# Masking of a key-value product: which side of the instruction has the stride

## The chip, the cores and the metric

The kernel runs on one core of one Trainium2 chip. The metric is the device time of one execution in microseconds; the time before is the median of three runs.

## What is computed

Two linear-attention blocks, A and B, read the same x (2048 rows of 640), and a gate mixes their outputs. There are 32 heads of width 20. Cut to what matters:

```
qkv = x @ wqkv                                     # per block, q, k, v of 32 heads
phi = lambda t: where(t > 0, t + 1, exp(t)) + 1e-6
pq, pk = phi(q), phi(k)
kv  = einsum("bhsd,bhse->bhde", pk, v)             # per head, 20 x 20
z   = einsum("bhsd->bhd", pk)
o   = einsum("bhqd,bhde->bhqe", pq, kv) / (pq . z + 1e-6)
out = g * (o_A @ wo_A) + (1 - g) * (o_B @ wo_B)    # g = sigmoid(sum(x * gate_w))
```

## The kernel before

All the work is listed as operations, each with an engine, a cost, its buffers and a priority, and a planner (`Sched`, from L105 on) lays them out by these costs; each engine then executes its list in that order, with semaphore waits between engines. The order of the PE products is written out by hand (`MAIN`), and the planner lets the query products fill in.

The kernel never forms v. It multiplies the key features with x itself (a matrix G of 640 x 640 for each block), and G with the value weights. The products of G and later those of the output use a scheme with seven half-size products for eight (steps numbered 1 to 7 in `MAIN`), so that the halves are combined by additions.

- **Keys** (L622, L623 on PE): projections of x, then exp and relu on ACT and the sum on DVE. L693 is one form of that sum: it reads PSUM as `p (m g) -> p g m` and writes runs of 128.
- **G** (`prod`, L889 on PE): five units G0 to G4. Each step is eight matmuls. ACT copies some results out (L918), DVE combines PSUM with a copy (`comb`, L923) into a tile, and writes the column for the denominator (`zsum`, L937, into `DEN`); its input is one float read 32 times, and it has a second scalar from PSUM. Step 4 of a unit writes into the bank that step 7's combine (called c22) and its z column have read, so it waits for both. A finished tile is transposed by a DMA of SP's queue into `GSA` or `GSB`.
- **Key-value product** (`kv_unit`, from L1003 on): for each block, matmuls (L1031) multiply the transposed G with the value weights. One result of a group of six heads has their value columns on its partitions and their 120 key columns along the row (24 values of m times 5 of g, key column 5m + g); of it only the blocks of a head with itself are wanted, so the mask depends on the partition and on m (the last group has two heads, 40 columns). DVE multiplies the PSUM result with a mask of zeros and ones (L1011) and writes the tile `KVL` in bf16. That is three instructions for each block: 480 elements a partition (four groups), 120 (one group) and 40 on 40 partitions.
- **Combined weights** (`wp_burst`, L1064 on PE): `KVL` times wo in two halves, called wA0, wA1, wB0 and wB1. Copies (L1080 on ACT, L1078 on DVE) take them to SBUF, and DMAs take them through DRAM into `WP`.
- **Queries** (L829 on PE, L854 and L856 on ACT, L859 and L866 on DVE): they fill PE's list between the others.
- **Denominators** (`den`, L1132 on PE, L1145 on DVE, L1155 and L1156 on ACT): the gated reciprocal for four blocks of 512 rows; four DMAs each spread it over partitions, and DVE multiplies the queries with it (L1183).
- **Output products** (L1250): scaled queries times `WP`, in the same seven-product scheme.

`MAIN` around the place of block A is `G3.6 G3.3 kvA G3.7 G4.1 G3.4 G4.2 wA0`. On DVE the three maskings of A come between the z column of G3.3 and c22 of G3.7 (L923), which its z column follows (L937). For block B it is `G4.4`, then query products, `kvB wB0 wB1`; the products of a denominator (L1132) and one more query unit stand on PE between kvB and wB0. On DVE the maskings of B come in front of L1145. wB0 waits for the maskings of B and for four loads of wo of B, which SP issues behind the stores and the reload of A's combined weights.

In `kv_unit` a column of PSUM is numbered by (group u, g, m), with m of 24 fastest and g of 5; the tile `KVL` has (u, m, g), with g fastest.

Of the kernel before, what the change touches and what calls it, by code (L numbers as in the profile page):

```python
# [15 lines left out]
NC = 5  # L16
# [88 lines left out]
class Sched:  # L105
# [8 lines left out]
    def op(self, eng, fn, cost, ins=(), outs=(), after=(), prio=None, name="", dma=None):  # L114
        if eng == "ACT" and dma is None:
            after = list(after) + self.consts
        o = Op(eng, fn, cost, list(ins), list(outs), after, (self.base or len(self.ops)) if prio is None else prio, name, dma)
        self.ops.append(o)
        return o
# [187 lines left out]
def body(nc, A_x, A_wqkv, A_wo, B_x, B_wqkv, B_wo, gate_w, out, log=None):  # L307
# [68 lines left out]
    WP, KVL = {}, {}  # L376
# [79 lines left out]
    def table(e):  # L456
# [8 lines left out]
            out=IDN[:, :], in_=ONE[:, 0:1].to_broadcast([128, 128]), pattern=[[-1, 128]], base=0, channel_multiplier=1, compare_op=ALU.is_equal, fill=0.0  # L465
# [334 lines left out]
    for i, X in enumerate(XS):  # L800
        src = (GI if i else GE)[:, :].rearrange("p (b s k) -> p k b s", b=NB, k=2)
# [201 lines left out]
    def kv_unit(X):  # L1003
        gv = GS[X][:, :, :].rearrange("p c (g m) -> p c g m", g=NC)

        def out(src, u0, n, w, mask, r0, r1):
            b = Buf("kvl")
            bkvl[X].append(b)
            op(
                "DVE",  # L1010
                lambda e: e.tensor_tensor(  # L1011
                    out=KVL[X][r0:r1, u0 : u0 + n, 0 : w * NC].rearrange("p u (m g) -> p u g m", g=NC),
                    in0=src().rearrange("p (u g m) -> p u g m", u=n, g=NC),
                    in1=mask.unsqueeze(1).unsqueeze(1).to_broadcast([r1 - r0, n, NC, w]),
                    op=ALU.mult,
                ),
                100 + 2.4 * w * NC * n,
                ins=[ps, bcst],
                outs=[b],
                prio=-1,  # L1020
                name="kvm",
            )

        for us in ((0, 1, 2, 3), (4, 5)):
            ps = Buf("kv", "ps")

            def fn(e, us=us, ps=ps):
                for i, u in enumerate(us):
                    for c in range(NC):
                        lo, n, w = (GR * u, 128, 24) if u < 5 else (540, 128, 8)  # L1030
                        r = e.matmul(  # L1031
                            PS[0:n, ps.slot, GR * i : GR * i + NC * w],
                            WV[X][:, c, lo : lo + n],
                            gv[:, c, :, 24 * u : 24 * u + w],
                            start=(c == 0),
                            stop=(c == NC - 1),
                        )
                return r

            o = op("PE", fn, 5 * len(us) * 55.0, ins=[bwv[X], bpad[X]] + [bgs[X, g] for g in range(NC)], outs=[ps], name="kv" + X)  # L1040
            kv_last[:] = [o]
            n = min(us[-1], 4) - us[0] + 1
            out(lambda ps=ps, n=n: PS[:, ps.slot, 0 : GR * n], us[0], n, 24, BDM, 0, 128)
            if 5 in us:
                out(lambda ps=ps: PS[64:104, ps.slot, GR : GR + 40], 5, 1, 8, BDE, 64, 104)
# [292 lines left out]
    for tok in MAIN.split():  # L1338
# [4 lines left out]
        if tok[0] == "G":  # L1343
            g, n = int(tok[1]), int(tok[3])
# [66 lines left out]
```

## Time and profile before

| | us |
|---|---|
| median of three runs | 183.12 (182.89 to 183.26) |
| the profiled execution | 182.12 |
| its span, from first to last instruction | 180.7 |
| PE busy in the span | 175.5 |
| DVE busy | 123.8 |
| ACT busy | 111.0 |

Time stamps are microseconds from the start of the span. A row of the timeline gives start, length, engine, line, operation, tiles (written <- read), shapes and count; in brackets stands the idle time ahead of it and what ended it. A row of a group gives the count, the total busy time and the mean length of one in ns, then the idle time ahead. A list of waits gives the total, the number and the longest wait. Matmuls overlap, and the end of one is modelled; from the start of one to the start of the next is the better measure of PE's pace. A few matmul records are missing in the trace, so a count can be one short.

### The profile page before, as it was taken

What the parts mean: (1) busy time and instruction counts of PE and PEld (TensorE: products, weight loads), DVE (VectorE), ACT (ScalarE), POOL (GpSimd) and SP (SyncE); (2) the same over time, 40 slices, a digit from 0 to 9 for tenths busy, and PEclk for the clock granted to TensorE, in tenths of its full rate; (3) what the DMA queues carried; (4) which work ended last, traced back from release to release, by engine and by line L of the source; (5) the groups of instructions that cost most, each with busy time, mean ns of one, the idle gap of its engine ahead of it and who ended that gap; (6) DMA issues with size and microseconds to landing.
All of it is one profiled execution on the core that took longest, in us unless ns stands there. A gap on an engine that the chain in (4) does not pass through costs nothing.

```text
span 180.7 us, 3303 instructions
## 1 busy us (share of the span) xinstructions
PE 175.5 (97%) x1283; PEld 108.6 (60%) x1297; DVE 123.8 (68%) x257; ACT 111.0 (61%) x219; POOL 4.5 (3%) x16
## 2 busy tenths in 40 slices
PE   8999999999999999999999997999999999999995
PEld 3555555555556776778565564555565666666662
DVE  2366969999999413315315479799999999695323
ACT  5289888899884321120395894699997565333340
POOL 1000000000000700000000000000000000000000
PEclk9999999999999999999999999999999999999999
DMA  7979999100000179832169592663200122421113
GB/s 198 302 141 170 227 378 364 46 2 0 4 0 0 36 150 287 102 73 40 19 199 221 178 191 36 163 169 97 58 4 0 43 88 78 121 82 69 56 60 109
DMA packets 33035, 20.60 MB, mean 114 GB/s; under 512 B 18260, under 2 KB 32892, under 8 KB 33020
## 3 DMA queue, kind: packets, MB, share of 16 engines
q1 hardware_dynamic: 32062, 19.76, 43.7%
q10 hardware_dynamic: 958, 0.63, 1.2%
q8 instruction: 10, 0.16, 0.4%
q14 instruction: 5, 0.04, 0.1%
HBM read 10.88 MB, written 4.26 MB: 84 GB/s over the span
## 4 chain that ended last, share of the span: by engine, by line
PE 85%; DVE 6%; DMA 4%; issue 2%; ACT 2%; SPq 1%; DVEq 0%
PE ps L889 20%; PE ps L1250 19%; PE ps L829 18%; PE ps L622 18%; PE ps L623 5%; DMA WKW<-WKW 2%; DVE PKS L1011 2%; DMA WKW<-in_A_wqkv_dram 2%; PE ps L1031 1%; SPq L421 1%; PE ps L1132 1%; ACT EQ L854 1%; PE ps L1064 1%; DVE PQ L1183 1%; DVE PKS L866 1%
## 5 line engine op out<-in xcount | busy, mean ns | idle before, releaser
L622 PE MATMUL ps<-WKW,XT 128*128 128x512 bf16 x154 | 42.8, 379 | 0.3 <-DMA WKW<-in_A_wqkv_dram 0.3
L623 PE MATMUL ps<-WKW,XT 128*128 128x128 bf16 (+1 forms) x160 | 35.1, 219 | 0.3
L854 ACT ACTIVATE EQ<-ps 128x512 bf16<-128x512 f32 x40 | 24.1, 601 | 9.0 <-PE ps L829 7.4
L622 PEld LDWEIGHTS ps<-WKW,XT 128*128 128x128 bf16 x160 | 15.6, 98 | 19.3 <-DMA WKW<-in_A_wqkv_dram 0.6
L668 ACT ACTIVATE EKT<-ps 128x640 bf16<-128x640 f32 x32 | 22.4, 705 | 6.4 <-PE ps L623 5.6
L889 PE MATMUL ps<-TX,PKS 128*128 128x321 bf16 (+1 forms) x160 | 24.8, 300 | 0.5 <-DVE DEN L937 0.4
L829 PE MATMUL ps<-XT,WQB 128*128 128x512 bf16 x95 | 23.2, 380 | 0.5 <-issue 0.4
L829 PE MATMUL ps<-XT,WQA 128*128 128x512 bf16 x97 | 22.2, 379 | 0.2
L923 DVE TENSOR_TENSOR WKW<-ps,EKT 128x320 bf16<-128x320 f32 x15 | 7.4, 492 | 21.4 <-PE ps L889 19.6
L889 PEld LDWEIGHTS ps<-TX,PKS 128*128 128x128 bf16 x160 | 15.1, 98 | 8.0 <-DVE DEN L937 1.5
L918 ACT ACTIVATE EKT<-ps 128x321 f32<-128x321 f32 (+1 forms) x15 | 6.6, 441 | 21.5 <-PE ps L889 21.3
L889 PE MATMUL ps<-XN,PKS 128*128 128x321 bf16 (+1 forms) x120 | 18.8, 299 | 0.0
L856 ACT ACTIVATE PKS<-ps 128x512 bf16<-128x512 f32 x30 | 18.0, 604 | 0.0
L829 PEld LDWEIGHTS ps<-XT,WQA 128*128 128x128 bf16 x100 | 11.7, 118 | 9.0
L829 PEld LDWEIGHTS ps<-XT,WQB 128*128 128x128 bf16 x100 | 11.4, 119 | 8.9 <-issue 0.6
L623 PEld LDWEIGHTS ps<-WKW,XT 128*128 128x128 bf16 x160 | 15.6, 98 | 0.0
L859 DVE TENSOR_SCALAR EQ<-EQ 128x512 bf16<-128x512 bf16 x40 | 10.8, 292 | 6.4 <-ACT EQ L854 6.0
L889 PEld LDWEIGHTS ps<-XN,PKS 128*128 128x128 bf16 x120 | 11.7, 98 | 5.1
L681 ACT ACTIVATE PKS<-ps 128x640 bf16<-128x640 f32 x20 | 14.0, 698 | 0.0
L866 DVE TENSOR_TENSOR PKS<-PKS,EQ 128x512 bf16<-128x512 bf16 x30 | 12.3, 423 | 1.6 <-ACT PKS L856 1.5
L732 DVE TENSOR_TENSOR PKS<-PKS 128x1280 bf16<-128x1280 bf16 (+1 forms) x20 | 13.0, 688 | 0.1
L1263 ACT ACTIVATE PKS<-ps 128x320 f32<-128x320 f32 x15 | 6.6, 440 | 9.3 <-PE ps L1250 9.3
(98 smaller groups left out, 217.9 us busy)
## 6 DMA issues: line engine op xcount, KB each, us to landing
out_dram<-PKS SPq DMA_DIRECT2D x15, 160.0 KB, 1.8
XN<-in_A_x_dram SPq DMA_DIRECT2D x1, 2240.0 KB, 9.3
WKW<-WKW SPq DMA_DIRECT2D x16, 64.0 KB, 2.1
WKW<-in_A_wqkv_dram SPq DMA_DIRECT2D x5, 160.0 KB, 3.6
WKW<-in_B_wqkv_dram SPq DMA_DIRECT2D x5, 160.0 KB, 3.7
WQA<-in_A_wqkv_dram SPq DMA_DIRECT2D x1, 800.0 KB, 10.9
WQB<-in_B_wqkv_dram SPq DMA_DIRECT2D x1, 800.0 KB, 13.4
WVA<-in_A_wqkv_dram SPq DMA_DIRECT2D x1, 800.0 KB, 9.9
```

The lines of the kernel that those rows point to most:

```text
L622: e.matmul(a[:, 0:512], l, WK[X][:, c, 0:512], start=(c == 0), stop=(c == NC - 1))
L623: return e.matmul(a[:, 512:w], l, WK[X][:, c, 512:w], start=(c == 0), stop=(c == NC - 1))
L668: op("ACT", lambda e, i=i, ps=ps: e.activation(evg(i), psg(ps), ACT.Exp), act_cost(D), ins=[ps] + first, outs=[ek, b], name="ke")
L681: op("ACT", lambda e, X=X, ps=ps: e.activation(pkt(X, t), psg(ps), ACT.Relu), act_cost(D), ins=[ps], outs=[rk], name="kr")
L732: op("DVE", lambda e: e.tensor_tensor(out=out, in0=a, in1=b, op=ALU.subtract), dve2(n * D), ins=ins, outs=[bb], name=name)
L829: r = e.matmul(PS[:, ps.slot + i, :], WQ[X][:, c, g::5], XT[:, c, 512 * b : 512 * b + 512], start=(c == 0), stop=(c == NC - 1),)
L854: op("ACT", lambda e: e.activation(ev(), pv(), ACT.Exp), act_cost(512 * n), ins=[ps], outs=[eq], name="qe")
L856: op("ACT", lambda e: e.activation(dst, pv(), ACT.Relu), act_cost(512 * n), ins=[ps], outs=[rq], after=pq_free.get((XS[slots[0] // NC], b) ...
L859: lambda e: e.tensor_scalar(ev(), ev(), 1.0, EPS, op0=ALU.min, op1=ALU.add),
L866: op("DVE", lambda e: e.tensor_tensor(out=dst, in0=dst, in1=ev(), op=ALU.add), dve2(512 * n), ins=[rq, eq, eq2], outs=[pq], name="qs")
L889: r = e.matmul(PS[:, ps.slot, 0:w], reg[:, j, :], mov(j, w), start=(first and j == 0), stop=(j == 7), skip_group_check=not first)
L1250: r = e.matmul(PS[:, ps.slot, 0:HALF], reg(g), mov(g), start=(first and g == 0), stop=(g == NC - 1), skip_group_check=not first)
```

## The change

The masking keeps its three instructions a block, its operands, its values and its declared cost; only the order in which each instruction goes through its elements changes. Before, PSUM is read as one run (u, g, m), and the tile is written with a step of five bf16 elements (10 bytes) inside rows of 24 or 8; the mask is read in rows of 24 or 8, the same row for every g. After, the tile is written as one run (u, m, g), PSUM is read in rows of five with a step of 24 floats (96 bytes; eight floats, 32 bytes, in the smallest one), and each mask element is read five times in a row.

```
                 lambda e: e.tensor_tensor(
-                    out=KVL[X][r0:r1, u0 : u0 + n, 0 : w * NC].rearrange("p u (m g) -> p u g m", g=NC),
-                    in0=src().rearrange("p (u g m) -> p u g m", u=n, g=NC),
-                    in1=mask.unsqueeze(1).unsqueeze(1).to_broadcast([r1 - r0, n, NC, w]),
+                    out=KVL[X][r0:r1, u0 : u0 + n, 0 : w * NC].rearrange("p u (m g) -> p u m g", g=NC),
+                    in0=src().rearrange("p (u g m) -> p u m g", u=n, g=NC),
+                    in1=mask.unsqueeze(1).unsqueeze(3).to_broadcast([r1 - r0, n, w, NC]),
                     op=ALU.mult,
```

The instructions of PE, ACT, POOL and SP and their order are the same in both kernels, and so is the order on DVE.

## Prediction

> **What bounds the kernel now.** I read the page's first two parts, then the PE waits, then the stretch around each of the two masking places.
>
> ```profile
> PE 175.5 (97%) x1283; PEld 108.6 (60%) x1297; DVE 123.8 (68%) x257; ACT 111.0 (61%) x219; POOL 4.5 (3%) x16
> PEclk9999999999999999999999999999999999999999
> ```
>
> PE is busy 97% of the span at full granted clock, and its order is fixed. The kernel ends when PE ends, so a faster DVE instruction pays only where PE stands still for it. The list of PE waits from 84 to 112 us names two real ones:
>
> ```profile
> PE ps L1064 <- DMA XN<-in_B_wo_dram: 0.7, 1, 0.7
> PE ps L889 <- DVE DEN L937: 0.4, 1, 0.4
> ```
>
> The masking (L1011) releases neither by name. The timeline of DVE shows what the second one really stands behind:
>
> ```profile
> 82.90 0.49 DVE L923 TENSOR_TENSOR WKW<-ps,EKT 128x320 bf16<-128x320 f32 x1 [2.79 <-PE ps L889]
> 83.42 0.26 DVE L937 SCALAR_TENSOR_TENSOR DEN<-EKT,ps,CST 128x32 bf16<-128x32 f32 x1
> 83.88 2.12 DVE L1011 TENSOR_TENSOR PKS<-ps,CST 128x480 bf16<-128x480 f32 x3 [0.20 <-PE ps L1031]
> 86.01 0.49 DVE L923 TENSOR_TENSOR WKW<-ps,EKT 128x320 bf16<-128x320 f32 x1
> 86.54 0.26 DVE L937 SCALAR_TENSOR_TENSOR DEN<-EKT,ps,CST 128x32 bf16<-128x32 f32 x1
> ```
>
> and the timeline of PE at the same time:
>
> ```profile
> 84.07 1.27 PE L889 MATMUL ps<-TX,PKS 128*128 128x321 bf16 x8
> 85.17 1.25 PE L889 MATMUL ps<-XN,PKS 128*128 128x321 bf16 x8
> 86.85 1.27 PE L889 MATMUL ps<-TX,PKS 128*128 128x320 bf16 x8 [0.43 <-DVE DEN L937]
> ```
>
> The three maskings of branch A hold DVE from 83.88 to 86.00. The c22 combine (L923) queued behind them needs the matmuls that start at 84.07 and end at 85.34; it starts only at 86.01. The z column (L937) follows it, and PE's G3.4, which overwrites the bank both of them read, waits for both until 86.85. Eight such matmuls take 85.17 − 84.07 = 1.10 us from start to start, so PE was ready at about 86.27: it loses 0.58 us (the 0.43 counts from a modelled end).
>
> **Removed and added.** Nothing is moved: PE, ACT, POOL and SP have the same instructions in the same order, and on DVE only the six maskings change their access patterns, at the same places. The groups of DVE by shape:
>
> ```profile
> L693 DVE SCALAR_TENSOR_TENSOR PKS<-ps,EKT 128x640 bf16<-128x640 f32 x12 | 9.9, 822 | 0.1
> L923 DVE TENSOR_TENSOR WKW<-ps,EKT 128x320 bf16<-128x320 f32 x15 | 7.4, 492 | 21.4 <-PE ps L889 19.6 <-ACT EKT L918 1.6
> L1011 DVE TENSOR_TENSOR PKS<-ps,CST 128x480 bf16<-128x480 f32 x2 | 3.0, 1511 | 0.3 <-PE ps L1031 0.2
> L937 DVE SCALAR_TENSOR_TENSOR DEN<-EKT,ps,CST 128x32 bf16<-128x32 f32 x10 | 2.6, 255 | 0.3
> L1145 DVE SCALAR_TENSOR_TENSOR WKW<-ps,EKT 128x256 f32<-128x256 f32 x4 | 1.7, 422 | 0.0
> L1011 DVE TENSOR_TENSOR PKS<-ps,CST 128x120 bf16<-128x120 f32 x2 | 1.2, 582 | 0.0
> L1011 DVE TENSOR_TENSOR PKS<-ps,CST 40x40 bf16<-40x40 f32 x2 | 0.5, 273 | 0.0
> ```
>
> What is the old price made of? L923 and L693 both read PSUM and write runs: (822 − 492) / 320 = 1.03 ns an element, and 492 − 330 = 162 ns fixed. At that rate 480, 120 and 40 elements would take 656, 286 and 203 ns. They take 855, 296 and 70 ns more: 1.8, 2.5 and 1.8 ns per element, but 43, 59 and 14 ns per inner row (20, 5 and 5 rows). The excess goes with the elements, not with the rows, and the one thing that differs for every element is the write that jumps 10 bytes. The old rate is (1511 − 582) / 360 = 2.58 ns, and the stretch of 2.12 us for 640 elements is 0.47 + 640 × 2.58 / 1000.
>
> The new instruction writes runs, reads PSUM at jumps of 96 bytes (24 floats) in rows of five, and reads each mask element five times (step 0). No row shows either form exactly.
> - PSUM jump: L693 reads PSUM at jumps of 20 bytes (five floats, the `m g` to `g m` view) at 1.03 ns, full rate. That is the lower bound; the upper one, from the only jump that this trace charges, is the old write's 1.55 ns extra.
> - Step 0: L937 reads one float 32 times. L1145 without its elements is 422 − 264 = 158 ns, so 32 elements should take 191; L937 takes 255. If step 0 carries all 64 ns, it is 2.0 ns an element; L937 also fetches a pointer scalar from PSUM, which may carry them instead, so the lower bound is nothing.
> - Below 1.03 ns there is no row that reads floats from PSUM, so I expect no further gain in the instruction itself.
>
> I take 1.03 ns, because L693 is nearest in all (PSUM read with jumps, runs written). The stretch is then 0.47 + 0.66 = 1.13 us, and DVE is free at 85.01.
>
> [...]
>
> **Place A, on the path.** c22 waits for its matmuls instead: they end at 85.34, and a combine starts 0.1 us behind them (matmuls end 82.78 to 82.80, L923 at 82.90), at 85.44. The z column starts 0.53 later, at 85.97, ends at 86.23, and PE follows 0.05 later: 86.28 against 86.85. **Gain 0.57 us**; PE's own stream (86.27) is the next limit. The masks may end as late as 85.42 for this, a stretch of 1.54 us or 1.67 ns an element; each further 0.1 ns costs 0.064 us, and at 2.58 ns nothing is left.
>
> **Place B, covered.** The maskings run 108.13 to 110.27, and wB0 (L1064) needs them. It waits longer for the last rows of wo of B:
>
> ```profile
> 109.32 1.03 PE L829 MATMUL ps<-XT,WQB 128*128 128x512 bf16 x4 [0.18 <-issue]
> 111.08 0.60 PE L1064 MATMUL ps<-XN,PKS 64*60 64x320 bf16 x15 [0.74 <-DMA XN<-in_B_wo_dram]
> ```
>
> DVE could release PE at 110.33; PE starts at 111.08. So a mask that ends at 109.26 buys nothing there. What stands behind it on DVE, the denominator (L1145, 110.31), can start at 109.2, when its own matmuls are done; its second ACT step (L1156) stands behind an exp (L854) that needs matmuls until 110.35, so the factor comes 0.6 us sooner, not 1.1. PE doesn't notice: from 112 to 131 it runs query matmuls (L829) with no named wait above 0.2. Without that cover it would be worth up to 0.6.
>
> The 0.57 must survive the DMA wait at B. Those loads are issued at 101.69 to 103.60, behind SP's reload of WP at 100.05, behind stores that wait for the copies of wA1 (ACT L1080, 93.05 and 93.90), which follow PE's wA1 at 91.97, after G3.4 in PE's order. Each link is started by the one before, so the landing should come 0.57 sooner with the rest.
>
> Sum: 182.12 − 0.57 = 181.55 for the profiled execution (span 180.7 and 1.4 around it). That execution lies 1.0 below the median of the runs, 183.12, so I forecast **182.55**. A measurement of this kernel can tell about 0.2% (0.37 us) from no change.
>
> **Rivals.**
> 1. *Forecast*, masks at 1.03 to 1.67 ns: 182.55. Chance 0.64.
> 2. *The read pays what the write paid* (PSUM jump at 2.58 ns, or step 0 at 1.03 + 2.0 = 3.03): stretch 2.12 to 2.41 us, time 183.12 to 183.41. [...] Against: L693. Chance 0.13, within 0.2%.
> 3. *The loads of wo for B don't come sooner*: PE gains 0.57 at A and stands 0.57 longer at wB0: 183.12. For: DMA engines are over 90% busy there from 101 to 109 us. Against: the chain of issues above. Chance 0.08.
> 4. *Slower: both charges add on every element*, 1.03 + 1.55 + 2.0 = 4.58 ns. Stretch 0.47 + 2.93 = 3.40 us: c22 1.28 us later at A, and at B the masks end at 111.53, past the DMA, 0.5 more at wB0: 183.12 + 1.78 = 184.9. It decides from 3.16 ns an element, where A loses 0.37. Against: two reads by separate operands would have to be charged in series. Chance 0.08.
> 5. *Place B pays too* (the wait put down to the DMA is really the mask's, or the landing comes earlier by itself): up to 0.9 us between 110.18, where the query matmuls leave PE free (109.32 and four times 0.216), and 111.08. 181.65. Chance 0.07.
>
> Faster 0.64 + 0.07 = 0.71; same 0.13 + 0.08 = 0.21; slower 0.08. The range goes from 182.1 (forecast, less 0.23 for the spread of the runs and 0.2 for a landing that moves) to 183.45 (rival 2's upper bound), and leaves out rivals 4 and 5, 0.15.
>
> **What would show it.** L1011 at about 660, 290 and 200 ns; c22 starting 0.1 after its matmuls; no PE wait for L937 near 86 us; the wait at wB0 still put down to the DMA, and wB0 near 110.5. L1011's 480 above 960 ns (1.67 × 480 + 162) would make the gain shrink, above 1.5 us would void it; a wait at wB0 grown by 0.5 would be rival 3.

## The result and the profile after

| | before | after |
|---|---|---|
| median of four runs, us | 183.00 (182.60 to 183.26) | 181.56 (181.50 to 182.03) |
| the profiled execution, us | 182.12 | 181.60 |
| its span, us | 180.7 | 180.2 |

The ratio is 0.9933, with an interval of 0.991 to 0.9956: 1.23 us faster, 0.81 to 1.65. The forecast was 182.55, a gain of 0.57 us, and the range ended at 182.1. The direction was right, the gain is about twice as large, and the time lies below the range.

The page's first part gives for each engine the busy time, its share and the instructions; the second fence holds what the list of PE waits from 84 to 112 us has left.

```profile
PE 177.0 (98%) x1297; PEld 109.1 (61%) x1297; DVE 121.8 (68%) x257; ACT 111.2 (62%) x219; POOL 4.5 (3%) x16
```

```profile
PE ps L1064 <- DMA XN<-in_B_wo_dram: 0.5, 1, 0.5
```

DVE has 2.0 us less to do, and the wait of G3.4 for the z column (L937) is gone. The wait of wB0 for the loads is shorter, 0.5 in place of 0.7, and still there. The groups of DVE by shape:

```profile
L1011 DVE TENSOR_TENSOR PKS<-ps,CST 128x480 bf16<-128x480 f32 x2 | 1.3, 658 | 0.3 <-PE ps L1031 0.2
L1011 DVE TENSOR_TENSOR PKS<-ps,CST 128x120 bf16<-128x120 f32 x2 | 0.5, 274 | 0.0
L1011 DVE TENSOR_TENSOR PKS<-ps,CST 40x40 bf16<-40x40 f32 x2 | 0.4, 202 | 0.0
```

(658 − 274) / 360 = 1.07 ns an element, in place of 2.58: at the price of a run (1.03 by the prediction's rows), so neither the PSUM jumps nor the mask elements read five times cost anything to speak of. At place A, the timeline of DVE, and below it that of PE:

```profile
84.41 1.06 DVE L1011 TENSOR_TENSOR PKS<-ps,CST 128x480 bf16<-128x480 f32 x3 [0.20 <-PE ps L1031]
85.97 0.49 DVE L923 TENSOR_TENSOR WKW<-ps,EKT 128x320 bf16<-128x320 f32 x1 [0.50 <-PE ps L889]
```

```profile
84.60 1.27 PE L889 MATMUL ps<-TX,PKS 128*128 128x321 bf16 x8
85.70 1.25 PE L889 MATMUL ps<-XN,PKS 128*128 128x321 bf16 x8
86.81 1.27 PE L889 MATMUL ps<-TX,PKS 128*128 128x320 bf16 x8
```

The maskings take 1.06 us and not 2.12; then DVE stands idle for 0.50 us and c22 (L923) waits for its matmuls. On PE the three starts are 1.10 and 1.11 apart: nothing is lost. All of it begins 0.53 later than in the profile of before, which is a matter of the start-up (see the table in the next section). At place B, the timeline of PE:

```profile
110.81 0.60 PE L1064 MATMUL ps<-XN,PKS 64*60 64x320 bf16 x15 [0.51 <-DMA XN<-in_B_wo_dram]
...
115.28 0.84 PE L1250 MATMUL ps<-PKS,PQ 128*128 128x320 bf16 x5
115.96 4.48 PE L829 MATMUL ps<-XT,WQA 128*128 128x512 bf16 x20
120.28 0.84 PE L1250 MATMUL ps<-GSB,XN 128*128 128x320 bf16 x5
```

Up to wB0 this agrees with the prediction: wB0 starts at 110.81 − 0.53 = 110.28 on the clock of before, against some 110.5. What it missed is in the profile of **before**, later. This is its chain of waits from 107 to 122 us, cut (start, length, what):

```profile
108.13 1.08 DVE PKS L1011
...
110.31 0.44 DVE WKW L1145
...
111.67 0.31 ACT WKW L1156
...
113.35 4.31 DMA WKW<-WKW
...
119.98 0.74 DVE XN L1216
...
120.77 0.85 PE ps L1250 x5
```

The chain of before goes through the maskings of B: behind them come the denominator (L1145), its reciprocal (L1155, L1156), the DMAs that spread it, the scaling of the queries (L1183) and a combine of scaled queries (L1216), and the output product that reads it (L1250 on `GSB` and `XN`; **Q** below) is what PE waits for. The timeline of PE in before hid that:

```profile
115.55 0.84 PE L1250 MATMUL ps<-PKS,PQ 128*128 128x320 bf16 x5
116.45 4.26 PE L829 MATMUL ps<-XT,WQA 128*128 128x512 bf16 x19
120.77 0.85 PE L1250 MATMUL ps<-GSB,XN 128*128 128x320 bf16 x5
```

No wait stands on the last line, and the prediction took that at its word. But the end of the row ahead of it is the modelled end of its last matmul. (That row counts 19 where after has 20. The record that is missing is the first: the row starts 0.90 us behind the product at 115.55, and in after 0.68 behind the one at 115.28, a difference of one matmul. So the last start can be read from it.) By the rows of PE one such matmul of 512 columns takes 0.38 us by itself, while the next one starts 0.216 behind it (a row of five takes 1.24, one of ten 2.32). The last of the 19 started at 116.45 + 4.26 − 0.38 = 120.33, so Q was due at 120.55, and it starts at 120.77: PE stood for 0.22 us, of which a count from the modelled end leaves 0.06. (At A the prediction had made just this correction, 0.43 to 0.58.) In after the last of 20 started at 115.96 + 4.48 − 0.38 = 120.06, and Q 0.22 later, at 120.28: it doesn't wait.

### The profile page after: what moved, and what is told of

Same layout as the page of the kernel before. It is cut to its first block, busy times and chain, and to the rows that moved or that the text cites. A ratio compares the mean times of both kernels' runs of the same rounds, so it can differ in the third digit from the quotient of the medians.

```text
span 180.2 us, 3317 instructions
## 1 busy us (share of the span) xinstructions
PE 177.0 (98%) x1297; PEld 109.1 (61%) x1297; DVE 121.8 (68%) x257; ACT 111.2 (62%) x219; POOL 4.5 (3%) x16
## 3 DMA queue, kind: packets, MB, share of 16 engines
HBM read 10.88 MB, written 4.26 MB: 84 GB/s over the span
## 4 chain that ended last, share of the span: by engine, by line
PE 90%; DMA 4%; DVE 2%; ACT 1%; SPq 1%; issue 1%; DVEq 0%
PE ps L889 22%; PE ps L1250 20%; PE ps L622 20%; PE ps L829 19%; PE ps L623 5%; DMA XN<-in_B_wo_dram 4%; PE ps L551 1%; PE ps L1064 1%; PE ps L1132 1%; SPq L421 1%; PE ps L1031 1%; ACT EQ L854 1%; PE ps L564 1%; DVE XT L1216 0%; DVE PKS L866 0%
## 5 line engine op out<-in xcount | busy, mean ns | idle before, releaser
L622 PE MATMUL ps<-WKW,XT 128*128 128x512 bf16 x160 | 44.4, 383 | 0.0
L622 PEld LDWEIGHTS ps<-WKW,XT 128*128 128x128 bf16 x160 | 15.8, 98 | 19.3 <-DMA WKW<-in_A_wqkv_dram 0.5
L829 PE MATMUL ps<-XT,WQB 128*128 128x512 bf16 x100 | 24.2, 380 | 0.0
L829 PE MATMUL ps<-XT,WQA 128*128 128x512 bf16 x100 | 22.9, 379 | 0.0
L923 DVE TENSOR_TENSOR WKW<-ps,EKT 128x320 bf16<-128x320 f32 x15 | 7.4, 491 | 21.9 <-PE ps L889 20.1
L866 DVE TENSOR_TENSOR PKS<-PKS,EQ 128x512 bf16<-128x512 bf16 x30 | 12.2, 419 | 1.6 <-ACT PKS L856 1.5
```

The lines of the kernel that those rows point to most:

```text
L622: e.matmul(a[:, 0:512], l, WK[X][:, c, 0:512], start=(c == 0), stop=(c == NC - 1))
L829: r = e.matmul(PS[:, ps.slot + i, :], WQ[X][:, c, g::5], XT[:, c, 512 * b : 512 * b + 512], start=(c == 0), stop=(c == NC - 1),)
L866: op("DVE", lambda e: e.tensor_tensor(out=dst, in0=dst, in1=ev(), op=ALU.add), dve2(512 * n), ins=[rq, eq, eq2], outs=[pq], name="qs")
```

## The experiments

**Theory.** The gain has two parts. At A it is the forecast 0.57. At B, Q starts at the later of two ways from kvB: through the loads of wo of B, wB0 and PE's own list; or through the maskings of B, L1145, the DMAs of the factor and L1216. Before, the second one ended last.

**Rivals.** B is worth something because the loads land sooner, or because wB0 itself comes sooner; or the whole gain is A's, and the rest is scatter; or the order of the maskings on DVE matters and not their price.

The table reads each profile by four starts on PE: kvA (first L1031 on `GSA`), kvB (first L1031 on `GSB`), wB0, and Q. All in us.

| kernel | start to kvA | kvA to kvB | kvB to wB0 | wB0 to Q | kvB to Q | profiled execution |
|---|---|---|---|---|---|---|
| before | 82.62 | 24.25 | 4.20 | 9.69 | 13.89 | 182.12 |
| before, again | 83.27 | 24.25 | 4.10 | 9.95 | 14.05 | 183.06 |
| A alone | 82.89 | 23.68 | 4.11 | 9.81 | 13.92 | 181.82 |
| old maskings, order of A | 83.66 | 23.69 | 3.90 | 10.17 | 14.06 | 182.74 |
| B alone | 83.38 | 24.25 | 4.26 | 9.46 | 13.72 | 182.68 |
| runs everywhere | 83.58 | 23.69 | 4.29 | 9.46 | 13.76 | 182.39 |
| after | 83.16 | 23.69 | 3.97 | 9.47 | 13.44 | 181.60 |
| after, again | 83.51 | 23.68 | 3.81 | 9.47 | 13.28 | 181.84 |
| before, wo of A | 83.05 | 24.25 | 3.44 | 10.58 | 14.02 | 182.9 |
| after, wo of A | 83.24 | 23.69 | 3.39 | 9.82 | 13.21 | 181.69 |
| before, order of B | 82.73 | 24.25 | 4.93 | 9.46 | 14.39 | 182.72 |
| after, wB0 later | 83.46 | 23.68 | 4.47 | 8.59 | 13.06 | 181.58 |

The second column has two values only, 24.25 and 23.68 to 23.69. The start-up scatters by 1.0 whatever the kernel, and the first profile of before has the lowest of all. From Q to the end of the span all these kernels take 59.93 to 60.06 us (60.2 in the two with wo of A, whose tail is longer), so what is gained at Q is gained at the end. The landing of the loads scatters too: where wB0 waits for them, it comes 3.81 to 4.29 us behind kvB, in old and new kernels alike. Every kernel with the old maskings of B ahead of L1145 has Q at 13.89 to 14.06 behind kvB, whenever wB0 came (3.44 to 4.20).

**Before, again.** The kernel of before unchanged, to see what two runs of one kernel differ by.

> The kernel before once more, for its spread. Theory: ratio 1.000; its profile starts about 0.5 us later than the profile of before (whose time, 182.12, lies 0.5 to 1.1 below its other runs), with the same three waits of PE, 0.58 near 86, about 0.9 at wB0 and 0.23 near 120.8. Rival 'the profile of before was ordinary and the runs without a profile are slower': the same start as before, and a profiled time again about 1 us below the median.

Ratio 1.0009 (0.9993 to 1.0024). Its profile is 0.94 us longer than the first one, 0.65 of it before kvA. Here Q stands behind L1216 for longer, and the list of PE waits names it:

```profile
PE ps L1064 <- DMA XN<-in_B_wo_dram: 0.6, 1, 0.6
PE ps L889 <- DVE DEN L937: 0.4, 1, 0.4
...
PE ps L1250 <- DVE XN L1216: 0.3, 1, 0.3
```

The third line is the wait that the first profile lacks: 0.3 from the modelled end, and 9.95 − 9.46 = 0.49 against PE's own list (9.46 behind wB0, in the lines of the table where Q doesn't wait). And a difference of two profiles, here 0.94 between equal kernels, isn't the change: the profiled 182.12 and 181.60 differ by 0.52 only because before had the short start-up.

**A alone, B alone.** The new access patterns in one block and the old ones in the other.

```
-   ....rearrange("p u (m g) -> p u m g", g=NC)
+   ....rearrange("p u (m g) -> p u m g" if X == "A" else "p u (m g) -> p u g m", g=NC)
    (the same choice for in0 and in1; "B" in the second kernel)
```

> Only block A's masks are turned round. Theory (three places: c22 behind the masks of A 0.57; the denominator behind the masks of B, which ends in a wait of PE near 120.8, 0.23; the rest of the measured gain is spread of the runs and of the landing of wo for B): 0.57 us faster than before, no PE wait near 86 us, PE still late by about 0.2 near 120.8. Rival 'place B pays at wB0': also about 0.5 here, with an unchanged wait at wB0. Rival 'all of the gain is place A': the whole 1.2 us.

> Only block B's masks are turned round. Theory: 0.23 us faster, from the wait of PE near 120.8 alone; the wait near 86 stays at 0.58 lost, the wait at wB0 stays put down to the DMA and within 0.25 of 0.9 lost. Rival 'place B pays at wB0': 0.6 to 0.9 faster, wB0's wait nearly gone. Rival 'all of the gain is place A': no change.

A alone: 182.15, ratio 0.9962 (0.9948 to 0.9977), 0.70 us (0.42 to 0.95). B alone: 182.42, ratio 0.9970 (0.9956 to 0.9984), 0.55 us (0.29 to 0.81), more than the 0.23 expected. The product of the two ratios is 0.9932, the whole change 0.9933. In the table A moves only kvA to kvB (0.57), and Q still waits 0.2 for L1216; B moves only kvB to Q, and Q waits no longer: 9.46 behind wB0 is PE's own list. In the profile of B alone wB0 waits 0.8 for its loads and comes 4.26 behind kvB, later than in before, and Q comes 0.17 to 0.33 sooner all the same. So wB0 isn't what this gain comes through. The trace accounts for 0.17 to 0.33 of the 0.55, which is inside the interval at its lower end. The rival "all of it is A's" falls.

**Old maskings, order of A.** Those of A are put behind the z column of G3.7; the price stays.

```
-   d["zb"] = zsum(two, px, t5, [d["c22"]])
+   d["zb"] = zsum(two, px, t5, [d["c22"]]); [setattr(k, "behind", d["zb"]) for k in kvm["A"] if g == 3]
```

> Masks as before; the three of block A stand behind c22 of G3.7 and its z column on DVE, with nothing else moved. Theory (what pays at A is what stands behind the masks, not DVE's time): 0.57 us faster, the masks still 1.5, 0.58 and 0.27 us and ending near 88.4, just ahead of wA0 at about 88.6. Rival 'the DVE time itself is what pays': no gain, or a loss at wA0.

Ratio 0.9974 (0.9961 to 0.9988), 0.48 us. The timeline of DVE at A:

```profile
87.01 0.26 DVE L937 SCALAR_TENSOR_TENSOR DEN<-EKT,ps,CST 128x32 bf16<-128x32 f32 x1
87.18 2.11 DVE L1011 TENSOR_TENSOR PKS<-ps,CST 128x480 bf16<-128x480 f32 x3
```

The maskings take 2.11 as before, and kvA to kvB is 23.69 as with the new maskings. At A the price mattered only because c22 was queued behind it. B keeps the old price and kvB to Q its old 14.06.

**Runs everywhere.** The tile is written in the order in which PSUM is read, so that both are runs; the columns of the tile are then in another order than the rest of the kernel wants.

```
-   out=....rearrange("p u (m g) -> p u m g", g=NC),
-   in0=....rearrange("p (u g m) -> p u m g", u=n, g=NC),
-   in1=mask.unsqueeze(1).unsqueeze(3).to_broadcast([r1 - r0, n, w, NC]),
+   out=....rearrange("p u (g m) -> p u g m", g=NC),
+   in0=....rearrange("p (u g m) -> p u g m", u=n, g=NC),
+   in1=mask.unsqueeze(1).unsqueeze(1).to_broadcast([r1 - r0, n, NC, w]),
```

> The masks read PSUM as one run and the mask in rows of 24, as before, but write the tile as one run in the order of PSUM. The tile's columns stand in the wrong order, so the output isn't the reference's. Theory (the jump of the write is the whole old price): 656, 286 and 203 ns for the three instructions. Rival (rows of 24 of the mask, or the row ends, carry it): 1.5 us, 0.58 and 0.27 stay.

658, 273 and 203 ns: the same as in after. With the read, the mask and the number of rows as in before, taking the jump out of the write alone takes the whole excess away. One run, 182.39; in its profile the loads landed late (wB0 at 4.29).

**Prices.** Extra products of 480 elements, PSUM times mask to bf16, twice each, from the place of B on: first with a write step of 1 to 8 elements, then written as a run with PSUM read in jumps or not and the mask with step 0 or not.

```
+   for st in (1, 2, 3, 4, 5, 6, 8):
+       d = PRC[:, 0 : 480 * st].rearrange("p (r m s) -> p r m s", r=20, s=st)[:, :, :, 0]
+       one(d, lambda: flat().rearrange(run, r=20), mrow)
+   one(d4, lambda: flat().rearrange(hop, u=4, g=NC), mone)
    (and three more: hop with a full mask; rows with mone, with a full mask)
```

> The kernel after, with 22 more instructions on DVE behind the first mask of B that multiply 480 floats of PSUM with a bf16 tile and write a part of SBUF that is free then, each started when the one before has ended; two rounds of: writes with a step of 1, 2, 3, 4, 5, 6 and 8 elements, then PSUM read with jumps of 96 bytes with and without step 0 on the second operand, then PSUM read as a run with and without step 0. The time has no meaning. [...] Rival theory (any write that isn't next to the last is charged): 660 at step 1 and 1.4 us at all the others. The four reads: 660 ns each; if step 0 or the jump costs something that the other hides, one of them is above 700.

Its time means nothing; the lengths do. The timeline of DVE, second round, at a step of 5 elements, and then PSUM in jumps with a mask of step 0:

```profile
132.78 1.47 DVE L1033 TENSOR_TENSOR PKS<-ps,CST 128x480 bf16<-128x480 f32 x1
...
138.51 0.65 DVE L1033 TENSOR_TENSOR PKS<-ps,CST 128x480 bf16<-128x480 f32 x1
```

| write step, bf16 elements | 1 | 2 | 3 | 4 | 5 | 6 | 8 |
|---|---|---|---|---|---|---|---|
| ns, first and second round | 648, 653 | 681, 689 | 962, 951 | 1215, 1208 | 1486, 1473 | 1752, 1749 | 2291, 2262 |

The four forms of the read took 651 to 653 ns: 96-byte jumps, with and without step 0, cost nothing. Of the write, the rival theory falls: the price isn't one for all jumps. A step of 3 already costs 0.3 us (956 ns, a run 651), and from a step of 2 on the length grows by about 270 ns for each further element, (2276 − 685) / 6 / 480 = 0.55 ns an element of the product and element of step.

**Prices, second.** Wider steps, float writes, strided bf16 reads of the second operand, and ACT, in the same manner.

```
+   for st in (1, 5, 10, 12):        add("DVE", ... out=wide(PRC, st, 0) ...)
+   for st in (1, 2, 4, 6):          add("DVE", ... out=wide(PRC.bitcast(f32), st, 0) ...)
+   for st in (1, 2, 4, 5, 8, 12):   add("DVE", ... in1=wide(XTf, st, 0) ...)
+   for st in (1, 2, 5, 8):          add("ACT", ... e.activation(wide(PRC, st, 0), ...))
```

> The kernel after, with 36 more instructions on 480 elements behind the first mask of B, one after the other, in two rounds; the time has no meaning. bf16 writes by DVE with steps of 1, 5, 10 and 12, float writes with steps of 1, 2, 4 and 6, bf16 reads from SBUF as the second operand with steps of 1, 2, 4, 5, 8 and 12, and ACT copies with bf16 write steps of 1, 2, 5 and 8. The writes by DVE measured so far cost 0.55 ns for each step of two bytes from step 2 on. Theory (the charge goes with the bytes that the write passes over): step 10 2.8 us, step 12 3.3 us, floats 660, 1200, 2270 and 3300 ns. Rival (it ends at a line of 16 bytes): all steps from 8 on, and floats from 4 on, 2.3 us. Reads from SBUF: 660 ns at all steps if they behave as those from PSUM; the writes' prices if the port is the cause. ACT: 570 ns at all steps, or the writes' prices as on DVE.

| ns for 480 elements, mean of two rounds | step in elements: length |
|---|---|
| DVE, bf16 write | 1: 652, 5: 1483, 10: 2294, 12: 2284 |
| DVE, float write | 1: 653, 2: 659, 4: 1024, 6: 1005 |
| DVE, bf16 read from SBUF | 1, 2 and 4: 650 to 651, 5: 675, 8: 1000, 12: 999 |
| ACT, bf16 write | 1: 568, 2: 722, 5: 1533, 8: 2330 |

All on DVE are flat from a step of 16 bytes to 24, the widest tried; ACT was not tried beyond 16. There a bf16 write costs 3.4 ns an element more than a run; a float write and a bf16 read only 0.7 to 0.8. Of the expectations, the end at 16 bytes is right, and 2.3 us for floats is wrong. On ACT a bf16 write pays much as on DVE, and more at a step of 2 (0.15 us more than a run, on DVE 0.03). Float writes and bf16 reads cost no more at a step of 8 bytes than as a run (659 and 651 ns), and more at 16 (1024 and 1000). The bf16 writes pay long before, 956 ns at 6 bytes. Why the charge stops growing at 16 bytes, no run shows.

**Loads of wo of B out of the way.** wB0 and wB1 use wo of A, which has long landed (in before its loads are issued from 65.6 to 67.3 us and take 8.7 at most), in the old and in the new kernel; block B's output is then multiplied with the weights of A. The four loads stay where they are, and SP waits for them at its end, which lengthens the tail by 0.24 us (from the start of PE's last matmul to the end 2.67 in place of 2.43).

```
-   WO[X][u][64 * r : 64 * r + w, lo + a : lo + b],
+   WO["A"][u][64 * r : 64 * r + w, lo + a : lo + b],
    (the waits of the matmuls on bwo["A", i] and bpo["A"])
```

> The kernel before, in which wB0 and wB1 multiply with wo of A, which has long been loaded, and so don't wait for the loads of wo for B (which still run); the output isn't the reference's. The order on every engine is the same. Theory (PE reaches the output product O5 near 120.8 us by the later of two ways: 9.46 us after wB0, or behind masks of B, denominator and factor, 13.9 to 14.05 us after the first matmul of kvB): wB0 starts 0.7 to 0.9 sooner, O5 waits for DVE that much longer, 13.9 to 14.05 us after kvB as before, and the time is that of before within 0.2. Rival (the two waits add): 0.7 faster than before.

> The same cut in the kernel after. Theory: wB0 follows its matmuls without a wait, 3.3 us after kvB; the way behind the masks is now at 13.1, so O5 comes 13.1 us after kvB in place of 13.44 to 13.76, 0.3 to 0.6 faster than the kernel after, about 181.1. Rival (the waits add, and the masks of B have no part): 0.7 to 0.9 faster than the kernel after.

In before: 183.26, ratio 1.0025 (1.0011 to 1.0038), 0.24 of the 0.46 being the tail; what is left, 0.22, is hardly more than the 0.2 that was expected at most. The wait at wB0 is gone, wB0 comes 0.66 to 0.76 sooner, and Q gains nothing:

```profile
110.74 0.60 PE L1064 MATMUL ps<-WOA,PKS 64*60 64x320 bf16 x15
...
115.54 0.85 PE L1250 MATMUL ps<-PKS,PQ 128*128 128x320 bf16 x5
...
121.32 0.85 PE L1250 MATMUL ps<-GSB,XN 128*128 128x320 bf16 x5 [0.61 <-DVE XN L1216]
```

What PE no longer waits at wB0 it waits later: 0.31 us at the output product of 115.54 (the row ahead of it starts at 114.12, and by before, where the two starts are 1.11 apart, it was due at 115.23), which reads queries that DVE has scaled with the factor (L1183), and 0.78 at Q, by the pace, in place of 0.22 and 0.49 in the two profiles of before. wB0 to Q has grown to 10.58. This is what decides against "the loads" and "wB0": with old maskings the way through the factor ends last, 14.0 behind kvB. In after: Q at 13.21 behind kvB with a wait of 0.2 for L1216, so the new maskings bring that way to about 13.2. On the clock 181.76, ratio 0.9949 (0.9931 to 0.9967); beside after's 0.9933 and 0.9942 the expected further 0.3 to 0.6 isn't seen, even with the tail taken off. By the traces Q comes only 0.07 to 0.23 sooner than in after, less than these intervals can tell: with the new maskings the two ways are nearly level.

**Before, order of B.** In the old kernel the maskings of B are put behind L1145, so that the factor's way loses them and wB0 gets them later.

```
-   span = sch.run()
+   span = sch.run(); [sch.order.remove(k) for k in kvm["B"]]; at = sch.order.index(stt_op[0]) + 1; sch.order[at:at] = kvm["B"]
```

> Masks as before; those of B stand behind the denominator (L1145) on DVE, with nothing else moved. Theory (the later of two ways decides): the denominator starts 1.0 us sooner, so the way behind it allows O5 at 13.1 us after kvB; but the masks now end 4.87 us after kvB and hold wB0, which starts at 4.9, and O5 comes 9.46 later, at 14.4, with no wait of its own: 0.3 to 0.5 slower than before. Rival (what pays at B is only what stands behind the masks, as at A): 0.4 to 0.6 faster.

183.18, ratio 1.0023 (1.0009 to 1.0038), 0.42 slower. The timeline of PE:

```profile
111.91 0.60 PE L1064 MATMUL ps<-XN,PKS 64*60 64x320 bf16 x15 [1.47 <-DVE PKS L1011]
...
121.38 0.84 PE L1250 MATMUL ps<-GSB,XN 128*128 128x320 bf16 x5
```

Now the first way is the later one: wB0 comes at 4.93, and Q 9.46 behind it, without a wait, as PE's list alone gives. Two ways and a maximum explain both orders; "the order matters, not the price" holds at A and falls at B.

**Other ways to use the time.** Three kernels on top of after that try to take away the wait of wB0 or give the planner the true price. WP's reload of A behind the loads of wo of B:

```
+   wpl["A0"].behind = [o for o in sch.ops if o.name == "wo2B"][0]
```

> The kernel after, with the reload of WP of A behind the four loads of wo for B in SP's queue; the planner moves a few query products and block B's products by this. Theory (the wait at wB0, 0.68 lost in the kernel after, is for the DMA): the loads land 2 to 4 us sooner, and the wait at wB0 goes; up to 0.7 faster than the kernel after if the later reload of WP holds nobody, 181.0. Rival: the reload then ends last, T1 (L1196) and the copies behind it on DVE wait, and PE loses the same near 115 to 121 us: 181.5 to 182.5.

The declared cost of the masking, and the declared rate of the loads:

```
-   100 + 2.4 * w * NC * n,
+   dve1(w * NC * n),
```

> The kernel after, with the declared cost of the masks set to that of a run (155 + 1.04 ns an element in place of 100 + 2.4), so that the planner lays out the operations behind block B anew. Theory (the order of PE hardly matters as long as it stands still only at wB0): within 0.3 us of the kernel after, 181.6. Rival: the new order starts the reciprocal and the copies of wB in a better order, and the wait near 120.8 keeps a margin: 0.2 to 0.7 faster than the kernel after.

```
-   rate=190.0,
+   rate=190.0 if X == "A" else 170.0,
```

> The kernel after, with the declared rate of the loads of wo for B at 170 in place of 190, by which the planner puts one more query product ahead of wB0. Theory: PE no longer stands still at wB0 (0.68 to 1.0 lost in the traces of the new masks); O5 is then set by the way behind the masks, 13.1 us after kvB, or by the later copies of wB: 0.3 to 0.6 faster than the kernel after, 181.1. Rival (as in the two other new layouts): what the planner moves on DVE and ACT makes the denominator late, and it is 0.5 slower than the kernel after.

Ratios to before: 0.9968 (0.9954 to 0.9982), 0.9998 (0.9983 to 1.0013) and 1.0068 (1.0041 to 1.0095); by their medians all three lose against after, though the interval of the first just meets after's. None came out as its theory had it (181.0, 181.6 and 181.1). In each the planner laid out other work anew. The first is rid of the wait at wB0 and waits 0.6 for L866 near a denominator product (L1132). With the true cost, the denominator went behind other DVE work, PE waits 0.7 at L1132, and nearly the whole gain of 1.2 us is gone. The third has the shortest kvB to Q of all, 12.86, and loses more later. Its twelve executions fall in two groups, six at a granted clock of PE of 1.00 (182.9 to 183.6) and six at 0.99 (184.4 to 185.1), so that the ratio is a mixture; already the first six, and the profile is one of them, are some 0.4 slower than before. Its PE waits:

```profile
PE ps L1132 <- DVE PKS L866: 2.5, 1, 2.5
```

Here a truer number in the planner made no better plan.

**After, again, and wB0 later.** After unchanged, and after with wB0 moved behind one more query product in PE's finished list, all other lists kept.

```
+   pe = [o for o in sch.order if o.eng == "PE"]; w = [o for o in pe if o.name == "wpB0"][0]; q = pe[pe.index(w) + 1]
+   sch.order.remove(w); sch.order.insert(sch.order.index(q) + 1, w)
```

> The kernel after once more. Theory: ratio 0.9933, the sum of A alone (0.9962) and B alone (0.9970); in the trace 23.69 us from kvA to kvB, and O5 9.46 us after wB0, 13.4 to 13.8 us after kvB. Rival (the first measurement took in a lucky set of runs): 0.996, what the trace of the first profile accounts for without the later start.

> The kernel after with wB0 behind one more query product on PE and nothing else moved in the order. Theory: PE doesn't wait for the loads of wo any more (wB0 at 4.4 us after kvB), O5 comes 8.39 us after it, at 12.9, or at 13.1 to 13.2, where the way behind the denominator ends: 0.3 to 0.5 faster than the kernel after, 181.2. Rival: ACT's copies of wB0 come 0.5 later and hold the exps behind them, or the later WP of B holds an output product: no gain, or a loss.

After: 181.89, ratio 0.9942 (0.9927 to 0.9956), 1.06 us. With wB0 later: 181.34, ratio 0.9912 (0.9896 to 0.9927), 1.6 us below before and 0.55 below after by the medians, the best of all. Its timeline of PE:

```profile
111.61 0.60 PE L1064 MATMUL ps<-XN,PKS 64*60 64x320 bf16 x15
...
120.21 0.84 PE L1250 MATMUL ps<-GSB,XN 128*128 128x320 bf16 x5
```

wB0 no longer waits, since a query product fills the time, and Q doesn't wait either: 13.06 behind kvB against 13.28. (wB0 to Q is 8.59, where 9.46 less five query matmuls of 0.216 would be 8.38: PE loses 0.2 ahead of wB1, which now stands closer behind wB0.) The 0.22 at Q is all of the 0.55 that the traces show; the rest stays open.

## Why the prediction was half right

- **The price of the masking** was right: 658, 274 and 202 ns against some 660, 290 and 200, a stretch of 1.06 against 1.13. Its reason was right too, the write's jump (runs everywhere: 658); the read is free (651 to 653). That the two charges add, rival 4, or that the read pays, rival 2, fell with it. (The range's end, 183.45, is called the bound of rival 2, whose own sum gives 183.41.)
- **Place A** was right to the hundredth: kvA to kvB went from 24.25 to 23.68, and c22 starts 85.97 − 0.54 = 85.43 on the clock of before (kvA is 0.54 later), predicted 85.44.
- **The gain survives the wait for the loads**: right. wB0 comes 3.81 and 3.97 behind kvB against 4.10 and 4.20, and with A alone 4.11: the loads come with the chain. That they come sooner still in after is not shown, since the landing scatters by 0.5.
- **Place B, covered**: this step failed. The working had the factor 0.6 us sooner and then said that PE doesn't notice, because no wait above 0.2 was named from 112 to 131. The factor itself was about right: L1156 starts 4.68 behind kvB in before (111.56) and 3.99 in after (110.83), 0.69 sooner. But PE did notice, because it did wait: 0.22 in the profile shown, hidden by a modelled end, and 0.49 in the second. Q came 13.89 and 14.05 behind kvB and now comes 13.44 and 13.28: **0.61** by the means, against nothing. Of this, 0.36 is the wait at Q that is gone, and 0.25 an earlier wB0, which may be scatter of the landing: the five profiles with the old maskings of B ahead of L1145 have Q at 13.99 on average, and the four with the new price in that place that only wait for their loads (B alone, runs everywhere, after twice) at 13.55, a difference of 0.44. A's 0.57 and these 0.4 to 0.6 make 1.0 to 1.2; the clock says 1.23 and 1.06. The cover by the wait at wB0 was real (0.5 us of it are still there), but it covered only one of two ways. Nor did the wait at wB0 cost before what its 0.7 said, since taking it away in the old kernel gained nothing.
- **Rival 5** gave nearly the measured time, 181.65, with a chance of 0.07, but for other causes, so that its nearness is luck. The wait at wB0 wasn't the mask's, and a landing earlier by itself would have helped nothing. The mechanism, the maskings ahead of the denominator, stood in the text of place B as "up to 0.6 without that cover", and the range left it out. With it as a case of its own the range would have reached 181.5.
- **From the profiled execution to the median**: subtracting from the median was right. The profile of before had the shortest start-up, 82.62 against 82.7 to 83.7 in the others; a forecast of 181.55 for the profiled execution and a measured 181.60 agree only because 0.53 of later start-up makes up for the 0.45 that these two profiles differ by at B, which is luck.

## What to carry to other kernels

Before an edit is costed at nothing because one wait covers it, follow the chain that ends last through that instruction: everything queued behind it on its engine has its own way back to the bound engine, and the later of two ways counts. A list of named waits isn't proof that the engine doesn't stand, since the modelled end of a pipelined matmul covers the first 0.16 us of a wait (0.38 less 0.216, at 512 columns): go from start to start, by the pace. Where VectorE takes PSUM to SBUF and one side must jump, give the stride to the read of PSUM, and write bf16 to SBUF as runs: 480 elements took 651 ns with the read in jumps of 96 bytes, and 1483 with the write in steps of 10 bytes.

## What the runs showed of the hardware

- A bf16 write of VectorE to SBUF pays for its step from 3 elements on, 0.55 ns an element for each further one up to 8, and no more at 10 and 12: for 480 elements 652, 685, 956, 1212, 1480, 1750 and 2277 ns at 1, 2, 3, 4, 5, 6 and 8, and 2294 and 2284 at 10 and 12. ACT is much alike, 568, 722, 1533 and 2330 at 1, 2, 5 and 8. Float writes and bf16 reads of VectorE cost no more at a step of 8 bytes than as a run (659 and 651 ns), and about 1000 ns at 16 and 24.
- VectorE reads floats from PSUM in 96-byte jumps, and a bf16 operand with step 0, as fast as runs: 651 to 653 ns for 480.
- The first matmuls of the keys (L622) ran at 0.38 us each from 3.52 us on in the first profile of before, but at 0.63 until 4.9 in after and until 5.9 with wB0 later, while the granted clock of the first 6 us is 1.00 in all three. It is part of the scatter of the start-up, 82.62 to 83.66 us. What decides it stays open.
